# Attention with top-32 masks and a gated product: the order and the engines of the weight decoding at the start, and the place of a small addition

## The chip, the cores and the metric

One core of a Trainium2 chip. The metric is the device time of one execution in microseconds (us); the median of three executions of the kernel before is 1266.33 us (1266.02 to 1269.22).

The engines are TensorE (PE in the rows, its weight loads PEld), VectorE (DVE), ScalarE (ACT), GpSimd (POOL) and SyncE (SP, which issues the DMAs). Each runs its own instructions strictly in the order in which the program lists them.

## What is computed

```
scores = q @ k.T / 8                       # 8 batches, 8 heads, 576 tokens, 64 wide
scores = where(scores >= 32nd largest of its row, scores, -1e9)
attn   = exp(scores - rowmax);  attn /= sum(attn) + 1e-9
x      = (attn @ v), heads side by side    # 4608 x 512
h      = (x @ w1) * (x @ w2) @ w3          # w1, w2: 512 x 1024, w3: 1024 x 1024
out    = h @ w_out                         # 1024 x 512
```

All of it is in 32-bit floating point.

## The kernel before, in words

**Slots.** The attention is cut into 144 slots, 18 to a batch; a slot is 128 query rows of two heads. Four consecutive rounds of the main loop (line 529) carry a slot: its scores (TensorE, `scores`), its search for the 32 largest (VectorE, `top32_steps`, tile `w` and `top`), its mask and exponentials (GpSimd and ScalarE, `edges_of`, `mask`, `exps`, tile `pab`), and its transposition and product with v (TensorE, `turn`, `values`). So in the round in which VectorE searches slot p, GpSimd and ScalarE mask slot p-1. In that round GpSimd forms the `edge` of slot p-1 first, then two subtractions on `pab`, then `over`, later the addition of 1e-9 to the two sums (`enlarge`, line 310, called at line 581), and, once VectorE has inverted the sums (`invert`), two multiplications (`normalise`). The next `edge` needs the end of VectorE's next search.

**Gated product.** The products with w1, w2 and the folded w3 @ w_out (`moe_steps`) are fed to TensorE in portions behind the attention, three portions in a round (`fill`, `SHARE`). Each product is made of three matmuls, from high parts and rests (`wh` and `wl` for w1 and w2, `wf` for the fold), since an fp32r operand carries only a high part. The evictions of a portion (`take_a`, `take_b`) come at the start of the next; the last of these is a subtraction on GpSimd into tile `g`.

**Weights.** The weights enter as 64-bit words in 40 units of 128 x 512: 8 of w_out, 16 of w3, 16 of w1 and w2. A unit is a generator of steps (`decode`, line 113). With `by_pool`, GpSimd first makes the sign bits (tile `y`); then ScalarE makes two conversions (`t`, into PSUM, and `r`, in the place of the word, tile `z`); then VectorE combines (SCALAR_TENSOR_TENSOR into `y`), preceded by the sign (TENSOR_SCALAR) where `by_pool` is false; then GpSimd adds (TENSOR_TENSOR into `y` or `wo`). A w1 or w2 unit goes on with the high part on ScalarE (`wh`, line 151) and the rest, `y` minus `wh`, on GpSimd (`wl`, line 153). A w3 unit waits for its four products with w_out (`product`, line 172, tile `pf`); after the second unit of a block ScalarE takes the high part and VectorE the rest (`wf`).

**What orders them.** `warm` (line 514) is called up to five times a round; a call is a turn. In a turn a new unit may enter if fewer than five are under way, and every unit under way takes its next step:

```
        if fetched and (n % 5 if n < 11 else n % 2) and len(going) < 5:
            z, step = fetched.pop(0)
            going.append(step(z))
        going[:] = [unit for unit in going if next(unit, "end") != "end"]
        prefetch(3)
```

`prefetch` issues the DMA of the next units on SyncE's queue, four buffers `z` in all. `weigh` (line 161) issues queued products of w3, 1 in the middle of a round and up to 8 at its end. The first portion of the gated product is issued once all 8 blocks of the fold and the first halves of w1 and w2 are in (`done`). In the kernel before, 12 of the 40 signs are made on GpSimd (those of every second unit of w_out and w3), and all 16 rests of w1 and w2.

A slot is numbered here by its place, 0 to 143. Slot k begins on VectorE with the first `w<-s,st`, and on GpSimd with its `edge`.

Of the kernel before, what the change touches and what calls it, by code (L numbers as in the profile page):

```python
# [9 lines left out]
F32 = mybir.dt.float32  # L10
# [4 lines left out]
ALU = mybir.AluOpType  # L15
# [6 lines left out]
NCC, NFC, NEC = DM // 128, DF // 128, DM // 128  # L22
# [13 lines left out]
STEEP = 2.0**80  # L36
SCALE = 0.125
AHEAD = 3
SHARE = 3520, 3520, 3200


# [19 lines left out]
def attn_moe(ctx: ExitStack, tc: tile.TileContext, q, k, v, w1, w2, w3, w_out, out, flag, general):  # L61
# [12 lines left out]
    pe, act, dve, pool, sp = nc.tensor, nc.scalar, nc.vector, nc.gpsimd, nc.sync  # L74
# [24 lines left out]
    wo = const.tile([128, NFC * DM], F32, tag="wl1", name="wo")  # L99
# [4 lines left out]
    if not general:  # L104
        pe, act, dve, pool, sp = (InOrder(tc, e) for e in (pe, act, dve, pool, sp))

    def fetch(src):

        z = z_p.tile([128, 1024], F32, tag="z", name="z")
        sp.dma_start(z.bitcast(I32), src)  # L110
        return z
# [27 lines left out]

    done = {"pf": 0, 0: 0, 1: 0}  # L140

    def load_w12(i, c, z):
        y = yield from decode(z, False)
        c, h = c // 2, c % 2
        if len(wl[i]) == h:
            while done["pf"] < NFC:
                yield
        if len(wl[i]) == h:
            wl[i].append(const.tile([128, half], F32R, tag="wl1", name="wl11"))
        y_hi, y_lo = wh[i][:, c * DF + h * 512 : c * DF + (h + 1) * 512], wl[i][h][:, c * 512 : (c + 1) * 512]  # L150
        act.copy(y_hi, y)
        yield
        pool.tensor_tensor(y_lo, y, y_hi.bitcast(F32), op=ALU.subtract)
        done[h] += 1

    def load_wout(c, z):
        yield from decode(z, c % 2, wo[:, c * 512 : (c + 1) * 512])

    fold, heavy = {}, []

    def weigh(n):
        while heavy and n:
            heavy.pop(0)()
            n -= 1

    def load_w3(c, z):
        f, i = c // 2, c % 2
        y = yield from decode(z, i)
        if i == 0:
            fold[f] = ps_m.tile([128, 512], F32, tag="mm", name=f"pf{f}")  # L170

        def product(j):
            pe.matmul(
                fold[f], y[:, (j % 4) * 128 : (j % 4 + 1) * 128], wo[:, j * DM : (j + 1) * DM],
                start=(j == 0), stop=(j == NFC - 1),
            )

        heavy.extend((lambda j=j: product(j)) for j in range(4 * i, 4 * i + 4))
        last = heavy[-1]
        if general:  # L180
            weigh(4)
        while last in heavy:
            yield
        if i == 1:
            cut = slice(f * DM, (f + 1) * DM)
            act.copy(wf[0][:, cut], fold[f])
            yield
            dve.tensor_tensor(wf[1][:, cut], fold[f], wf[0][:, cut].bitcast(F32), op=ALU.subtract)
            done["pf"] += 1
# [120 lines left out]
    def enlarge(sums):  # L310
        pool.tensor_scalar(sums, sums, 1e-9, None, op0=ALU.add)
# [56 lines left out]
    def moe_steps(b, part, xs, after):  # L368
# [57 lines left out]
            after(lambda p=p, e=e: take_o(p, e))  # L426
            yield cost

    outs_w = [(w_out[c], lambda z, c=c: load_wout(c, z)) for c in range(8)]
    thirds = [(w3[c], lambda z, c=c: load_w3(c, z)) for c in range(2 * NFC)]  # L430
    firsts = [
        (w[2 * c + h], lambda z, i=i, c=2 * c + h: load_w12(i, c, z))
        for h in range(2) for i, w in enumerate((w1, w2)) for c in range(NCC)
    ]
    startup = outs_w[:4] + thirds[:1] + outs_w[4:] + thirds[1:2]
# [1 line left out]
        startup += firsts[f - 1 : f] + thirds[2 * f : 2 * f + 2]  # L437
    startup += firsts[NFC - 1 :]

    def new_x():  # L440
        return x_p.tile([128, 2, NA], F32R, tag="x", name="xf")

    if general:
        for src, step in startup:
            for _ in step(fetch(src)):
                pass
        with tc.For_i(0, B, 1) as b:
            seen = small.tile([1, 1], I32, tag="seen", name="seen", bufs=1)
            nc.sync.dma_start(seen, flag[ds(b + 1, 1), :])
            with tc.If(nc.values_load(seen, min_val=0, max_val=1) > 0):  # L450
                for part in range(2):
                    qk, vts, xs = {}, {}, {}
                    for of, hps, t in SLOTS:
                        if of != part:
                            continue
                        for hp in hps:
                            if hp not in qk:
                                qk[hp], vts[hp], xs[hp] = load_qk(b, part, hp), load_v(b, hp), new_x()
                        s, st = new_s(), scores([qk[hp] for hp in hps], t)
                        for h in range(2):  # L460
                            take_scores(s, st, h)
                        edge = top32_exact(s)
                        pab, sums = new_weights()
                        for a in range(2):
                            mask(s, edge, pab, a)
                            exps(edge, pab, sums, a)
                        enlarge(sums)
                        invert(sums)
                        normalise(pab, sums)
                        tp, ro = turn(pab)  # L470
                        ov = values([vts[hp] for hp in hps], t, *take_turned(tp, ro), ro)
                        to = places([xs[hp] for hp in hps], t)
                        take_high(to, ov)
                        take_low(to, ov)
                    for _ in moe_steps(b, part, [xs[hp] for hp in range(NHP)], lambda f: f()):
                        pass
        return
# [26 lines left out]
                spare -= cost  # L504

    waiting = list(startup)
    fetched, going, turns = [], [], []

    def prefetch(n):
        while waiting and len(fetched) < n:  # L510
# [3 lines left out]
    def warm(first=True):  # L514

        if p < 0 and not first:
            return
        turns.append(p)
        n = len(turns)
        if fetched and (n % 5 if n < 11 else n % 2) and len(going) < 5:  # L520
            z, step = fetched.pop(0)
            going.append(step(z))
        going[:] = [unit for unit in going if next(unit, "end") != "end"]
        prefetch(3)

    qk[units[0]] = load_qk(*units[0])
# [1 line left out]
    n_slots = len(slots)  # L528
    for p in range(-1, n_slots + 3):
        i, j, m = p + 1, p - 1, p - 2  # L530
        if i < n_slots:
            for u in units:
                if first[u] - 2 == i:
                    qk[u] = load_qk(*u)
                if first[u] == i:
                    vts[u] = load_v(u[0], u[2])
        finder = top32_steps(ss[p], *sts.pop(p), p) if 0 <= p < n_slots else iter(())
        if 0 <= j < n_slots:
            edges[j] = edges_of(j)
        next(finder, None)  # L540
        if m - 1 in lows:
            take_low(*lows.pop(m - 1))
            b, part, _ = slots[m - 1][0][0]
            if final[b, part] == m - 1:
                queue.append(moe_steps(b, part, [xts.pop((b, part, hp)) for hp in range(NHP)], put_off.append))
        next(finder, None)
        if p >= 0:
            warm()
        if 0 <= j < n_slots:
            pabs[j] = new_weights()  # L550
            for a in range(2):
                mask(ss[j], edges[j], pabs[j][0], a)
            compare(j)
        fill(SHARE[0])
        next(finder, None)
        if 0 <= m < n_slots:
            tp, ro = turn(pabs[m][0])
            pts, pr = take_turned(tp, ro)
        warm(False)
        if 0 <= j < n_slots:  # L560
            exps(edges[j], *pabs[j], 0)
            exps(edges[j], *pabs[j], 1)
        weigh(1)
        fill(SHARE[1])
        next(finder, None)
        warm(False)
        if i < n_slots:
            st = scores([qk[u] for u in slots[i][0]], slots[i][1])
            ss[i] = new_s()
            take_scores(ss[i], st, 0)  # L570
            sts[i] = st, take_scores(ss[i], st, 1)
        if 0 <= m < n_slots:
            us, t = slots[m]
            for u in us:
                if u not in xts:
                    xts[u] = new_x()
            ov = values([vts[u] for u in us], t, pts, pr, ro)
            lows[m] = places([xts[u] for u in us], t), ov
            take_high(*lows[m])
        if 0 <= j < n_slots:  # L580
            enlarge(pabs[j][1])
        next(finder, None)
        warm()
        next(finder, None)
        if 0 <= j < n_slots:
            invert(pabs[j][1])
            normalise(*pabs[j])
        weigh(8)
        fill(SHARE[2])
        for _ in finder:  # L590
            pass
        if 0 <= m < n_slots:
            del ss[m], pabs[m], edges[m]
        warm()
# [62 lines left out]
```

## Time and profile before

| | |
|---|---|
| median of three executions | 1266.33 us |
| profiled execution, its own time | 1266.87 us |
| its span, first to last instruction | 1264.9 us |
| mean granted clock of TensorE | 0.991 of full speed |
| busy TensorE / VectorE / ScalarE / GpSimd | 1209.7 / 1135.0 / 943.4 / 872.4 us |
| TensorE in 40 slices of 31.6 us, busy tenths | 3788889999..., and 9 in nearly all slices after |
| slot 0 begins on VectorE, slot 18 | at 9.57 us, at 208.15 us |

A busy tenth of 9 means 90% or more. Busy matmul time is modelled to the end of the pipeline, so a slice in which TensorE shows 8 may hold real gaps. In the tables of groups, a row gives engine, operation, output and inputs, sizes and count, then busy us in all and mean ns of one, then the engine's idle time just before them and what ended it.

### The profile page before, as it was taken

The page shows a single profiled execution, that of the slowest core. Times are in us where ns is not written, and L with a number is a line of the kernel's source. Part 1 is how long each engine was busy: PE and PEld are TensorE (multiplying, and loading weights), DVE is VectorE, ACT ScalarE, POOL GpSimd, SP SyncE. Part 2 cuts the span into 40 slices and gives each one's busy share as a digit, 9 for nine tenths or more (in the row PEclk, how much of TensorE's full clock was granted, in tenths as well). Part 3 has the DMA queues.
Part 4 walks back from the last instruction along what each step waited for, and adds up shares of the span by engine and source line. Part 5 has one row for each costly group of instructions (what it writes and reads, how often), then busy time and mean ns, then how long its engine had stood idle before and what let it go on. Part 6 is the DMA issues. An engine that isn't in the chain of part 4 may idle for free.

```text
span 1264.9 us, 29916 instructions
## 1 busy us (share of the span) xinstructions
PE 1209.7 (96%) x10513; PEld 1043.5 (82%) x10513; DVE 1135.0 (90%) x3968; ACT 943.4 (75%) x2025; POOL 872.4 (69%) x1213
## 2 busy tenths in 40 slices
PE   3788889999999999999999999999999999999998
PEld 1444568888888888888888888888888888888898
DVE  7897979999999999999999999999999999999910
ACT  5887877777777777777777777777777777777731
POOL 5887887676766767676766767676766767676731
PEclk9999989999999999999999999999999999999999
DMA  7533421202112121202112121202112111202000
GB/s 236 174 129 130 156 70 40 91 27 70 55 39 90 36 63 40 90 28 70 55 39 91 36 63 40 90 28 70 55 39 91 35 63 40 91 27 70 13 22 21
DMA packets 42803, 85.92 MB, mean 68 GB/s; under 512 B 4754, under 2 KB 21138, under 8 KB 42642
## 3 DMA queue, kind: packets, MB, share of 16 engines
q1 hardware_dynamic: 42642, 83.91, 20.6%
q8 instruction: 85, 1.39, 0.5%
q14 instruction: 76, 0.62, 0.2%
HBM read 74.45 MB, written 9.44 MB: 66 GB/s over the span
## 4 chain that ended last, share of the span: by engine, by line
PE 75%; POOL 10%; DVE 7%; ACT 4%; issue 3%; DMA 1%; SPq 0%; DVEq 0%; POOLq 0%; ACTq 0%
PE ab L52 27%; PE eo L52 15%; PE ro L52 12%; PE st L52 11%; PE tp L52 9%; POOL pab L52 5%; DVE w L52 3%; DVE top L52 2%; ACT pab L52 2%; PE pf L52 2%; POOL y L52 2%; POOL g L52 1%; DVE y L52 1%; POOL wl L52 1%; ACT pts L52 1%
## 5 line engine op out<-in xcount | busy, mean ns | idle before, releaser
L52 POOL TENSOR_TENSOR pab<-s,pab 128x576 f32<-128x576 f32 x288 | 404.8, 1427 | 121.9 <-ACT pab L52 121.9
L52 DVE MAX8 top<-w 128x8 f32<-128x192 f32 (+1 forms) x1152 | 478.5, 448 | 0.0
L52 PE MATMUL ab<-xf,wh 128*128 128x256 f32 (+1 forms) x2048 | 438.5, 302 | 10.1 <-DVE y L52 8.7
L52 PEld LDWEIGHTS ab<-xf,wh 128*128 128x128 f32 x2048 | 332.9, 189 | 21.6 <-DVE y L52 9.5
L52 ACT ACTIVATE pab<-s,edge 128x576 f32<-128x576 f32 x288 | 208.0, 769 | 176.6 <-POOL edge L52 176.6
L52 PE MATMUL ab<-xf,wl 128*128 128x256 f32 (+1 forms) x1024 | 307.4, 300 | 0.0
L52 DVE MATCH_REPLACE8 w<-top,w 128x192 f32<-128x192 f32 x864 | 289.7, 343 | 0.0
L52 POOL TENSOR_SCALAR pab<-pab,sums 128x576 f32<-128x576 f32 x288 | 212.6, 751 | 78.0 <-DVE sums L52 78.0
L52 ACT ACTIVATE pab<-pab,edge 128x576 f32<-128x576 f32 x288 | 223.1, 779 | 11.9 <-POOL pab L52 9.7
L52 PE MATMUL eo<-g,wf 128*128 128x256 f32 (+1 forms) x1536 | 231.6, 301 | 0.0
L52 PEld LDWEIGHTS eo<-g,wf 128*128 128x128 f32 x1536 | 208.5, 188 | 8.1 <-issue 7.5
L52 PEld LDWEIGHTS ab<-xf,wl 128*128 128x128 f32 x1024 | 193.4, 189 | 4.1 <-issue 4.1
L52 PE MATMUL st<-kt,qt 64*128 64x192 f32 (+3 forms) x1280 | 182.8, 435 | 9.8 <-DMA kt<-in_k 4.8
L52 ACT COPY pts<-tp 128x1024 f32<-128x1024 f32 x144 | 145.6, 1011 | 46.8 <-PE tp L52 44.3
L52 ACT COPY s<-st 128x768 f32<-128x768 f32 (+1 forms) x288 | 169.9, 646 | 5.8 <-PE st L52 5.8
L52 PE MATMUL tp<-ident,pab 128*128 128x128 f32 x1152 | 153.8, 278 | 14.2 <-DVE w L52 9.5
L52 PEld LDWEIGHTS st<-kt,qt 64*128 64x128 f32 (+1 forms) x1280 | 97.9, 178 | 83.7 <-issue 18.6
L52 DVE TENSOR_TENSOR w<-w,st 128x384 f32<-128x384 f32 x288 | 158.2, 549 | 4.9
L52 PE MATMUL ro<-pts,vt 128*64 128x128 f32 (+1 forms) x2560 | 161.2, 269 | 1.0 <-ACT pr L52 1.0
L52 DVE TENSOR_TENSOR w<-s,st 128x384 f32<-128x384 f32 x288 | 146.7, 551 | 14.0
L52 POOL TENSOR_TENSOR g<-whole,g 128x256 fp32r<-128x256 f32 (+1 forms) x128 | 103.3, 807 | 78.6 <-ACT g L52 78.6
L52 PEld LDWEIGHTS ro<-pts,vt 128*64 128x64 f32 x2560 | 127.5, 137 | 34.4 <-issue 24.2
(47 smaller groups left out, 1128.7 us busy)
## 6 DMA issues: line engine op xcount, KB each, us to landing
vt<-in_v SPq DMA_DIRECT2D x64, 352.0 KB, 3.2
kt<-in_k SPq DMA_DIRECT2D x64, 320.0 KB, 3.8
z<-in_w SPq DMA_DIRECT2D x32, 512.0 KB, 3.8
qt<-in_q SPq DMA_DIRECT2D x32, 160.0 KB, 3.2
out_t<-osb SPq DMA_DIRECT2D x32, 160.0 KB, 1.8
z<-in_wo SPq DMA_DIRECT2D x8, 512.0 KB, 5.2
qt<-in_q SPq DMA_DIRECT2D x32, 128.0 KB, 3.1
out_t<-osb SPq DMA_DIRECT2D x32, 128.0 KB, 1.7
```

The source lines that it names most:

```text
L52: ins = fn(*args, **kw)
```

## The change

The turns in which a unit enters are read from a list of ones and zeros, one digit a turn; a second list says for each unit, in its order of entry, whether GpSimd makes its sign (29 ones of 40); a third says for each unit of w1 and w2 whether VectorE makes its rest (12 ones of 16). The order of the units is changed at two places and among the last nine. In the middle of a round 2 queued products of w3 are issued in place of 1. The addition of 1e-9 to the sums is called right behind the exponentials, ahead of the evictions of the second portion and of two turns that stood before it.

```diff
+ENTER = "011111010110010011111101000100110101111011001101110111011111000111100010000101010101010101010101010101010101010101010101"
+BY_POOL = "1111011100011100111001110101011111111111"
...
-    def load_w12(i, c, z):
-        y = yield from decode(z, False)
+    def load_w12(i, c, z, by_pool, rest):
+        y = yield from decode(z, by_pool)
...
-        pool.tensor_tensor(y_lo, y, y_hi.bitcast(F32), op=ALU.subtract)
+        (dve if rest else pool).tensor_tensor(y_lo, y, y_hi.bitcast(F32), op=ALU.subtract)
...
-    def load_wout(c, z):
-        yield from decode(z, c % 2, wo[:, c * 512 : (c + 1) * 512])
+    def load_wout(c, z, by_pool):
+        yield from decode(z, by_pool, wo[:, c * 512 : (c + 1) * 512])
...
-    def load_w3(c, z):
+    def load_w3(c, z, by_pool):
...
-        y = yield from decode(z, i)
+        y = yield from decode(z, by_pool)
...
-        (w[2 * c + h], lambda z, i=i, c=2 * c + h: load_w12(i, c, z))
+        (w[2 * c + h], lambda z, s, i=i, c=2 * c + h: load_w12(i, c, z, s, '1101011101011111'[8 * h + 4 * i + c // 2] == "1"))
...
+    startup = [startup[i] for i in [0, 1, 2, 3, 4, 5, 6, 7, 8, 9, 11, 10, 12, 13, 14, 16, 15, 17, 18, 19, 20, 21, 22, 23, 24, 25, 26, 27, 28, 29, 30, 31, 33, 35, 32, 38, 39, 37, 34, 36]]
...
-        if fetched and (n % 5 if n < 11 else n % 2) and len(going) < 5:
+        if fetched and ENTER[n : n + 1] != "0" and len(going) < 5:
             z, step = fetched.pop(0)
-            going.append(step(z))
+            by_pool = BY_POOL[len(entered)] == "1"
+            entered.append(n)
+            new = step(z, by_pool)
...
             exps(edges[j], *pabs[j], 1)
-        weigh(1)
+            enlarge(pabs[j][1])
+        weigh(2)
         fill(SHARE[1])
...
-        if 0 <= j < n_slots:
-            enlarge(pabs[j][1])
         next(finder, None)
```

How this moves instructions is shown at three places. The first is VectorE at the start of the program, up to the search of slot 0 (`top_98` is the tile of slot 0's largest values, `y` and `t` belong to weights). Before:

```order
L52 TENSOR_SCALAR y<-t 128x512
L52 SCALAR_TENSOR_TENSOR y<-t,y 128x512
L52 TENSOR_TENSOR w<-s,st 128x2x192 x2
L52 TENSOR_TENSOR w<-w,st 128x2x192 x2
L52 MAX top_98<-w 128x8 x2
```

Now:

```order
L54 TENSOR_TENSOR w<-s,st 128x2x192 x2
L54 TENSOR_TENSOR w<-w,st 128x2x192 x2
L54 SCALAR_TENSOR_TENSOR y<-t,y 128x512
L54 MAX top_98<-w 128x8 x2
L54 MATCH_REPLACE w<-top_98,w 128x192 x2
```

The sign of the first unit is gone from VectorE, and its combination stands behind the first four operations of the search.

The second is GpSimd in slot 11, from its edge to the next (`wl` is a rest of w1, TENSOR_SCALAR `y<-z` a sign, TENSOR_TENSOR `y<-y,z` the addition of a unit). Before:

```order
L52 TENSOR_TENSOR edge<-top_100,coef 128x4
L52 TENSOR_TENSOR wl_107<-y,wh_101 128x512
L52 TENSOR_TENSOR y<-y,z 128x512
L52 TENSOR_TENSOR pab<-s,pab 128x576 x2
L52 TENSOR_TENSOR over<-top_100 128x2
L52 TENSOR_TENSOR wl_107<-y,wh_101 128x512
L52 TENSOR_TENSOR y<-y,z 128x512
L52 TENSOR_SCALAR sums<-sums 128x2
L52 TENSOR_SCALAR pab<-pab,sums 128x576 x2
L52 TENSOR_TENSOR wl_107<-y,wh_101 128x512
L52 TENSOR_TENSOR y<-y,z 128x512
L52 TENSOR_TENSOR edge<-top_98,coef 128x4
```

Now:

```order
L54 TENSOR_TENSOR edge<-top_100,coef 128x4
L54 TENSOR_SCALAR y<-z 128x512
L54 TENSOR_TENSOR pab<-s,pab 128x576 x2
L54 TENSOR_TENSOR over<-top_100 128x2
L54 TENSOR_TENSOR wl_107<-y,wh_101 128x512
L54 TENSOR_SCALAR y<-z 128x512
L54 TENSOR_SCALAR sums<-sums 128x2
L54 TENSOR_SCALAR y<-z 128x512
L54 TENSOR_TENSOR y<-y,z 128x512
L54 TENSOR_SCALAR y<-z 128x512
L54 TENSOR_SCALAR pab<-pab,sums 128x576 x2
L54 TENSOR_TENSOR y<-y,z 128x512
```

Three rests and three additions have become one rest, two additions and four signs.

The third is GpSimd in slot 15, after the last weights. Before:

```order
L52 TENSOR_TENSOR edge<-top_98,coef 128x4
L52 TENSOR_TENSOR pab<-s,pab 128x576 x2
L52 TENSOR_TENSOR over<-top_98 128x2
L52 TENSOR_TENSOR g<-whole,g 128x320
L52 TENSOR_SCALAR sums<-sums 128x2
L52 TENSOR_SCALAR pab<-pab,sums 128x576 x2
```

Now:

```order
L54 TENSOR_TENSOR edge<-top_98,coef 128x4
L54 TENSOR_TENSOR pab<-s,pab 128x576 x2
L54 TENSOR_TENSOR over<-top_98 128x2
L54 TENSOR_SCALAR sums<-sums 128x2
L54 TENSOR_TENSOR g<-whole,g 128x320
L54 TENSOR_SCALAR pab<-pab,sums 128x576 x2
```

The addition to the sums has passed the subtraction into `g`.

## Rows read from the trace of the kernel before

**Rows 1.** The page: busy time, and TensorE in 40 slices.

```profile
PE 1209.7 (96%) x10513; PEld 1043.5 (82%) x10513; DVE 1135.0 (90%) x3968; ACT 943.4 (75%) x2025; POOL 872.4 (69%) x1213
...
PE   3788889999999999999999999999999999999998
```

**Rows 2.** Windows: stretch and length, busy PE, PEld, DVE, ACT, POOL, granted clock, DMA.

```profile
9.57:192.35 182.78, 143.17 (x844) 88.50 (x845) 162.99 (x494) 140.03 (x276) 151.53 (x175) 0.94 0.43 142
600.00:640.00 40.00, 40.00 (x340) 35.39 (x338) 37.84 (x133) 31.29 (x68) 28.82 (x41) 1.00 0.17 53
1220.00:1240.00 20.00, 20.00 (x161) 19.94 (x160) 2.51 (x7) 4.34 (x11) 2.94 (x4) 1.00 0.05 19
```

**Rows 3.** Timeline of VectorE: start, length, operation, idle before and its end.

```profile
8.24 0.69 DVE L52 TENSOR_SCALAR y<-t 128x512 int32<-128x512 int32 x1 [8.24 <-ACT t L52]
...
9.57 1.01 DVE L52 TENSOR_TENSOR w<-s,st 128x384 f32<-128x384 f32 x2
...
20.24 1.01 DVE L52 TENSOR_TENSOR w<-s,st 128x384 f32<-128x384 f32 x2
...
49.93 0.69 DVE L52 SCALAR_TENSOR_TENSOR y<-t,y 128x512 int32<-128x512 int32 x1 [2.47 <-POOL y L52]
...
53.24 1.01 DVE L52 TENSOR_TENSOR w<-s,st 128x384 f32<-128x384 f32 x2
```

**Rows 4.** Timeline of ScalarE at the start.

```profile
6.50 1.18 ACT L52 COPY s<-st 128x768 f32<-128x768 f32 x2 [4.49 <-PE st L52]
7.57 0.64 ACT L52 ACTIVATE t<-z 128x512 f32<-128x512 f32 x1
...
8.68 0.62 ACT L52 ACTIVATE t<-z 128x512 f32<-128x512 f32 x1
```

**Rows 5.** Groups of VectorE, by form, from 0 to 200 us.

```profile
L52 DVE SCALAR_TENSOR_TENSOR y<-t,y 128x512 int32<-128x512 int32 x40 | 27.6, 689 | 6.6 <-POOL y L52 3.2 <-ACT xf L52 2.5
L52 DVE TENSOR_SCALAR y<-t 128x512 int32<-128x512 int32 x28 | 19.1, 683 | 14.1 <-ACT t L52 13.9
...
L52 DVE TENSOR_TENSOR wf<-pf,wf 128x512 fp32r<-128x512 f32 x8 | 5.5, 686 | 1.3 <-ACT wf L52 1.3
```

**Rows 6.** Groups of GpSimd, by form, from 0 to 200 us.

```profile
L52 POOL TENSOR_TENSOR pab<-s,pab 128x576 f32<-128x576 f32 x32 | 44.6, 1416 | 8.1 <-ACT pab L52 8.1
L52 POOL TENSOR_TENSOR y<-y,z 128x512 int32<-128x512 int32 x32 | 41.5, 1298 | 1.3 <-ACT z L52 1.1
...
L52 POOL TENSOR_TENSOR wl<-y,wh 128x512 fp32r<-128x512 f32 x16 | 20.5, 1280 | 4.7 <-ACT wh L52 4.7
...
L52 POOL TENSOR_SCALAR y<-z 128x512 f32<-128x512 f32 x12 | 7.9, 660 | 8.1 <-DMA z<-in_wo 8.1
...
L52 POOL TENSOR_TENSOR over<-top 128x2 f32<-128x2 f32 x16 | 3.2, 200 | 0.0
```

**Rows 7.** Timeline of GpSimd: the edges of slots 11 and 14.

```profile
145.21 0.20 POOL L52 TENSOR_TENSOR edge<-top,coef 128x4 f32<-128x4 f32 x1
...
185.01 0.21 POOL L52 TENSOR_TENSOR edge<-top,coef 128x4 f32<-128x4 f32 x1
```

**Rows 8.** Groups of ScalarE, by form, from 0 to 200 us: an exponential has two instructions.

```profile
L52 ACT ACTIVATE pab<-pab,edge 128x576 f32<-128x576 f32 x32 | 24.7, 775 | 4.5 <-POOL pab L52 4.1
...
L52 ACT ACTIVATION_READ_ACCUMULATOR pab<-pab,edge 128x1 f32 x32 | 6.2, 193 | 0.0
```

**Rows 9.** Waits of VectorE and GpSimd in slots 0 to 15: us in total, times, longest.

```profile
DVE y L52 <- ACT t L52: 5.7, 4, 2.3
...
DVE y L52 <- POOL y L52: 3.2, 2, 2.5
...
POOL sums L52 <- ACT pab L52: 2.0, 5, 0.8
```

**Rows 10.** Waits from 240 to 1160 us.

```profile
DVE sums L52 <- POOL sums L52: 21.7, 40, 0.9
...
PE tp L52 <- DVE w L52: 0.7, 4, 0.2
```

More of the change, by code (lines that the diff above doesn't have):

```diff
@@ L427, in moe_steps @@
             yield cost
-    outs_w = [(w_out[c], lambda z, c=c: load_wout(c, z)) for c in range(8)]
-    thirds = [(w3[c], lambda z, c=c: load_w3(c, z)) for c in range(2 * NFC)]
+    outs_w = [(w_out[c], lambda z, s, c=c: load_wout(c, z, s)) for c in range(8)]
+    thirds = [(w3[c], lambda z, s, c=c: load_w3(c, z, s)) for c in range(2 * NFC)]
     firsts = [
-        (w[2 * c + h], lambda z, i=i, c=2 * c + h: load_w12(i, c, z))
+        (w[2 * c + h], lambda z, s, i=i, c=2 * c + h: load_w12(i, c, z, s, '1101011101011111'[8 * h + 4 * i + c // 2] == "1"))
         for h in range(2) for i, w in enumerate((w1, w2)) for c in range(NCC)
@@ L444, in attn_moe @@
         for src, step in startup:
-            for _ in step(fetch(src)):
+            for _ in step(fetch(src), False):
                 pass
@@ L506, in attn_moe @@
     waiting = list(startup)
-    fetched, going, turns = [], [], []
+    fetched, going, turns, entered, begun = [], [], [], [], []
     def prefetch(n):
@@ L519, in warm @@
         n = len(turns)
-        if fetched and (n % 5 if n < 11 else n % 2) and len(going) < 5:
+        if fetched and ENTER[n : n + 1] != "0" and len(going) < 5:
             z, step = fetched.pop(0)
-            going.append(step(z))
-        going[:] = [unit for unit in going if next(unit, "end") != "end"]
+            by_pool = BY_POOL[len(entered)] == "1"
+            entered.append(n)
+            new = step(z, by_pool)
+            if False:
+                next(new)
+                begun.append(new)
+            else:
+                going.append(new)
+        going[:] = [unit for unit in going if next(unit, "end") != "end"] + begun
+        begun.clear()
         prefetch(3)
```

## The prediction, made before the changed kernel was run

> **What bounds the kernel now.** I read the page first. TensorE is busy in nearly every slice but the first six; all its missing tenths lie in the first 190 us, the stretch in which weights enter [rows 1]. The windows say what that means on either side. Between 600 and 640 us TensorE is busy 40.00 of 40.00 us while VectorE has 37.84 and GpSimd 28.82, and near the end TensorE works alone, 20.00 of 20.00 [rows 2]. After the weights TensorE is therefore the bound, and from 240 to 1160 us the trace has 0.7 us in which it waited for anything [rows 10]. In the first stretch, 9.57 to 192.35 us, no engine is full: of 182.78 us VectorE is busy 162.99, GpSimd 151.53, TensorE 143.17, ScalarE 140.03 [rows 2]. Sixteen slots take these 182.78 us, 11.4 each, against 7.9 later. Nothing but the first stretch can pay. Since both programs begin the gated product in the same slot, with the same number of matmuls in each slot and in the tail, a microsecond saved before TensorE fills up is a microsecond off the end.
>
> In that stretch VectorE and GpSimd are tied to each other twice a slot: GpSimd's edge needs VectorE's last search step, and VectorE's inversion needs the sums from GpSimd. So a slot takes about the longer of the two engines' work, plus what the ties leave open: VectorE has 182.78 - 162.99 = 19.8 us open, in waits such as 5.7 us for ScalarE's `t` and 3.2 us for a sign from GpSimd [rows 2, 9].
>
> **The change part by part.**
>
> *Work moved.* 17 signs leave VectorE at 0.683 us and come to GpSimd at 0.660: -11.6 and +11.2. 12 rests leave GpSimd at 1.280: -15.4. What a rest costs on VectorE no row shows. The nearest row is the rest of the fold, same shape and same subtraction on the same engine, with one input from PSUM: 0.686 us. The far bound is GpSimd's own 1.280 [rows 5, 6]. I take 0.69, since engine and operation are the same, so +8.3 on VectorE, and keep 1.28 for the range. In all GpSimd loses 4.2 us and VectorE 3.3 in a stretch where both are nearly full. The rest of the forecast is about where that work lies.
>
> *A, slots 0 to 3.* VectorE now waits 8.24 us for the first `t`, makes a sign and a combination, and begins the search at 9.57 [rows 3]. In the changed order the search stands first, and the score copies that it needs end at 6.50 + 1.18 = 7.68 [rows 4]: -1.9. Slot 0 then holds six weight operations as before, and may keep its 10.67 us (20.24 - 9.57). Slot 1 holds three in place of five: two at 0.65 (between a row's mean and its pace back to back), -1.3. In slot 3 VectorE waited 2.47 us for a sign that GpSimd had reached late [rows 3]; of the two units with a sign from GpSimd that slot 3 combines now, one has it ahead of the masks and the other is combined one search step later, so -2.5. Against this, ScalarE gets a fifth pair of conversions ahead of the scores of slot 1; a pair takes 8.68 - 7.57 = 1.1 us [rows 4], +1.1. Sum: **-4.6**, to be seen at the start of slot 4, now 53.24. The cautious end is what GpSimd's own work in slots 0 to 2 loses: from 4 signs, 9 additions, 1 rest to 5 signs and 8 additions, 0.66 - 1.30 - 1.28 = -1.9.
>
> *B, slots 3 to 10.* GpSimd's list goes from 6 signs, 20 additions, 7 rests (38.9 us with rows 6) to 14, 22 and 2 (40.4): **+1.5**. VectorE's list stays at 41 or 42 weight operations. This is where the saving of signs is paid back.
>
> *C, slots 11 to 13.* From the edge of slot 11 to that of slot 14 passed 185.01 - 145.21 = 39.8 us [rows 7]. GpSimd had 7 additions and 8 rests there, 7 x 1.30 + 8 x 1.28 = 19.3 us; now 5 signs, 5 additions, 2 rests, 12.4 us. That is -6.9. In the last of the three, VectorE's search beside it (7.5 without weights, 37.84 us of 40 in a slot of 7.9, and one rest) is then longer than GpSimd's 7.1 by 1.1. **-5.8**.
>
> *D, the addition to the sums.* It now stands right behind the exponentials. GpSimd must wait for the second of them, 0.775 + 0.193 us after the last mask, less the 0.20 of `over`, so 0.8 us [rows 6, 8], wherever no operation of a weight stands between. That is so in four of slots 0 to 13 (1, 3, 6, 13): +3.2, where 2.0 us were waited before [rows 9]: **+1.2**. Behind it now queue the subtraction into `g` and the steps of two turns, which get later by no more; their readers are turns away. In the other 130 slots the same move is put at nothing: it shortens VectorE's wait for the sums (21.7 us from 240 to 1160), but TensorE covers all of that, and if it did not, 21.7 us would be the gain [rows 10].
>
> *At nothing.* Two products in mid-round in place of one: their number is the same, and TensorE has 39.6 us open in the stretch [rows 2]. Were it not covered, one product more in mid-round would hold up scores, not the sum. SyncE's queue: the loads of q and k stand behind one load of weights less; the loads of weights wait for a free `z` as before, and the first addition, which frees one for the fifth unit, is delayed by little more than the two signs that now stand ahead of it (1.3 us).
>
> Sum: -4.6 + 1.5 - 5.8 + 1.2 = **-7.7 us**. The profiled execution took 1266.87, the median 1266.33, 0.5 less; I put the sum on the median: **1258.6 us**.
>
> **The rivals.**
>
> *Slower: the two engines shut each other out.* Of VectorE's operations in the stretch, none subtracts or compares two tensors that both lie in SBUF; each has PSUM on one side or a single input. The moved rest reads `y` and `wh`, both in SBUF, while GpSimd is busy 83% of the time reading SBUF. If the two cannot read together, a rest waits for half of GpSimd's operation in flight, up to 1.416 / 2 = 0.71 us [rows 6], and GpSimd then stands for 0.69: 1.4 x 12 = 16.8 us, all on the path if neither engine has room. -7.7 + 16.8 = +9.1, **1275.4 us**. It decides from 0.64 us lost per rest. No row of before has such an operation, so the trace neither shows nor excludes it. For it speaks that both engines are nearly full; against it that VectorE and GpSimd have 20 and 31 us open in the stretch, in which part of such waits would fall, and that the twelve rests are spread over nine slots.
>
> The Trainium skill (SBUF — State Buffer, "Who interferes with whom") says just this: a VectorE instruction with two SBUF inputs contends with a GpSimd instruction that reads SBUF, and the second to issue waits until the first is finished. By that page the sum would be the rival's, +9.1, where the row of the fold's rest gives -7.7; no run here shows it yet.
>
> *No change that can be told: a rest costs what it cost GpSimd, and A stays small.* With 1.28 in place of 0.69 a rest costs 7.1 us more in all, half of it in slots where VectorE is the longer, 3.5; and A is only GpSimd's -1.9, because ScalarE or the loads hold up the start. -1.9 + 1.5 - 5.8 + 1.2 + 3.5 = -1.5, **1264.8 us**. For it speaks that slot 2 now holds more of GpSimd's work (3 signs and 4 additions) than before.
>
> *Much faster: VectorE runs without gaps.* If the new order also fills the 19.8 us, VectorE's load alone is the limit: -19.8 - 3.3 = -23.1, **1243.2 us**. Against it: its waits come from ScalarE and GpSimd alike [rows 9], and in some slots four pairs of conversions, 4 x 1.1 us, now stand on ScalarE.
>
> *The change does nothing:* if a unit of the last list were still needed later than before, the gated product would begin later. It begins in the same slot, so this has no chance of its own.
>
> **How the numbers follow.** A difference of 0.3%, 3.8 us, is about what a measurement of this kernel can tell from no change. Forecast as worked out, faster by 4 to 15 us: 0.58. Much faster: 0.11. No change: 0.17. Shut out, or another mishap above +3.8: 0.14. So faster 0.69, same 0.17, slower 0.14. The range reaches below to half of VectorE's gaps, -7.7 - 9.9 and the 1.9 by which A might be larger, near **1247**; above it takes in the rival of no change with its bound and part of the way to the slower one, **1269**. Left out are most of the slower rival and the end of the fastest case.
>
> **What would show it.** In the profile of the changed kernel: slot 4 begins on VectorE near 48.6 us (A); the edges of slots 11 and 14 lie 34 us apart (C); VectorE's rest takes about 0.69 us and GpSimd's operations keep their lengths (against the slower rival); TensorE is full from about 185 us, and the tail is the same. The forecast is wrong if the rests on VectorE show 1 us or more or a wait for GpSimd in front of each, if GpSimd's subtractions on `pab` lengthen beyond 1.42 us, if VectorE's wait for signs grows well beyond 3.2 us, or if TensorE waits after 200 us.

## The result, and the profile after

The changed kernel takes **1247.44 us** (median of four executions, 1246.48 to 1248.36), the kernel before 1266.70 beside it: ratio 0.9844, interval 0.9827 to 0.9861. That is faster by 19.3 us. The forecast was 7.7 us, that is 1258.6; the time lies in the range (1247 to 1269) at its lower end, and the size of the gain was wrong by more than half.

The profiled execution took 1246.48 us, with a span of 1244.6 where before it was 1264.9. The page answers to [rows 1], and its chain of work is given for the first time here:

```profile
PE 1202.3 (97%) x10513; PEld 1042.5 (84%) x10513; DVE 1137.1 (91%) x3963; ACT 941.0 (76%) x2025; POOL 869.4 (70%) x1218
...
PE   4889799999999999999999999999999999999998
...
PE 91%; DVE 3%; POOL 2%; ACT 2%; issue 1%; DMA 1%; SPq 0%; ACTq 0%; DVEq 0%
```

In the kernel before, that chain ran 75% over TensorE, 10% over GpSimd and 7% over VectorE. The windows answer to [rows 2]: the first stretch, slots 0 to 15 by their starts on VectorE, and the same 40 us later:

```profile
6.86:177.71 170.85, 138.45 (x836) 86.31 (x837) 164.23 (x490) 141.51 (x280) 150.72 (x181) 0.96 0.47 157
...
600.00:640.00 40.00, 40.00 (x356) 35.53 (x352) 38.74 (x137) 31.26 (x68) 28.69 (x42) 1.00 0.16 49
```

The stretch is 11.9 us shorter, yet VectorE's work in it grew from 163.0 to 164.2 us. What went are VectorE's open times: 170.85 - 164.23 = 6.6 us, before 19.8. From 600 to 640 us TensorE shows 40.00 of 40.00 busy, to the digit what it showed before.

The starts of slots on VectorE and the edges on GpSimd answer to [rows 3, 7]. VectorE:

```profile
6.86 1.02 DVE L54 TENSOR_TENSOR w<-s,st 128x384 f32<-128x384 f32 x2 [6.86 <-ACT s L54]
...
47.91 1.01 DVE L54 TENSOR_TENSOR w<-s,st 128x384 f32<-128x384 f32 x2
...
177.71 1.02 DVE L54 TENSOR_TENSOR w<-s,st 128x384 f32<-128x384 f32 x2
...
1175.10 1.02 DVE L54 TENSOR_TENSOR w<-s,st 128x384 f32<-128x384 f32 x2
```

GpSimd, slots 11 and 14:

```profile
138.01 0.20 POOL L54 TENSOR_TENSOR edge<-top,coef 128x4 f32<-128x4 f32 x1
...
171.21 0.20 POOL L54 TENSOR_TENSOR edge<-top,coef 128x4 f32<-128x4 f32 x1
```

From slot 16 to slot 143 (the last of these starts) pass 997.4 us, and 1003.4 before: 6.0 us less, in a part of the program in which nothing but the place of the small addition changed.

The groups of VectorE and GpSimd from 0 to 200 us answer to [rows 5, 6]. VectorE, with the rests that it now makes:

```profile
L54 DVE TENSOR_TENSOR wl<-y,wh 128x512 fp32r<-128x512 f32 x12 | 13.3, 1110 | 0.1
...
L54 DVE TENSOR_TENSOR wf<-pf,wf 128x512 fp32r<-128x512 f32 x8 | 5.5, 682 | 0.0
```

GpSimd:

```profile
L54 POOL TENSOR_TENSOR pab<-s,pab 128x576 f32<-128x576 f32 x36 | 51.6, 1458 | 6.9 <-ACT pab L54 6.9
...
L54 POOL TENSOR_TENSOR over<-top 128x2 f32<-128x2 f32 x18 | 5.4, 297 | 0.0
...
L54 POOL TENSOR_TENSOR wl<-y,wh 128x512 fp32r<-128x512 f32 x4 | 5.2, 1288 | 0.0
```

A rest on VectorE takes 1.11 us on average, not 0.69, and GpSimd's operations beside it are longer: `pab` 1.458 (1.416 before), `over` 0.297 (0.200).

The waits from 7 us to slot 16 answer to [rows 9]. VectorE:

```profile
DVE w L54 <- ACT s L54: 6.9, 1, 6.9
DVE y L54 <- ACT t L54: 3.5, 6, 1.0
DVE y L54 <- POOL y L54: 0.8, 1, 0.8
DVE sums L54 <- POOL sums L54: 0.6, 1, 0.6
```

GpSimd:

```profile
POOL sums L54 <- ACT pab L54: 5.9, 9, 1.7
```

The wait for `s` is the one ahead of slot 0. GpSimd waits 5.9 us for exponentials (before 2.0), more than the 3.2 forecast for the moved addition, but VectorE does not feel it: its own wait for the sums is 0.6 us here and was 3.7 in the same slots before.

### The profile page after: what moved, and what is told of

The parts are those of the page before. It is cut to its first block, busy times and chain, and to the rows that moved or that the text cites. A ratio compares the mean times of both kernels' runs of the same rounds, so it can differ in the third digit from the quotient of the medians.

```text
span 1244.6 us, 29906 instructions
## 1 busy us (share of the span) xinstructions
PE 1202.3 (97%) x10513; PEld 1042.5 (84%) x10513; DVE 1137.1 (91%) x3963; ACT 941.0 (76%) x2025; POOL 869.4 (70%) x1218
## 4 chain that ended last, share of the span: by engine, by line
PE 91%; DVE 3%; POOL 2%; ACT 2%; issue 1%; DMA 1%; SPq 0%; ACTq 0%; DVEq 0%
PE ab L54 33%; PE eo L54 17%; PE ro L54 15%; PE st L54 13%; PE tp L54 10%; PE pf L54 3%; POOL pab L54 1%; DVE w L54 1%; DVE top L54 1%; DVE y L54 1%; DVE wl L54 1%; POOL y L54 1%; ACT pab L54 0%; POOL wo L54 0%; ACT s L54 0%
## 5 line engine op out<-in xcount | busy, mean ns | idle before, releaser
L54 PEld LDWEIGHTS tp<-ident,pab 128*128 128x128 f32 x1152 | 133.8, 142 | 24.7 <-POOL pab L54 15.4
```

The costliest lines, as they stand in the source:

```text
L54: ins = fn(*args, **kw)
```

## Experiments

Three questions came from this. Why do the later slots gain? Why did VectorE's waits vanish? What lengthens the rests? Two theories stand in several expectations. **P** says that the place of the addition pays in every slot after the weights, behind a TensorE that only looks full. **M** says that the list of turns and the list of signs fit each other, so that either without the other loses. Each expectation spells out its theories and rivals. "After" is the changed kernel.

### The place of the addition

*e1: the kernel before with this edit alone.*

```diff
             exps(edges[j], *pabs[j], 1)
+            enlarge(pabs[j][1])
...
-        if 0 <= j < n_slots:
-            enlarge(pabs[j][1])
```

> The kernel before with one edit, the addition of 1e-9 called right behind the exponentials. Theory P (place): in the slots after the weights the change made a slot 7.864 us long in place of 7.899, because the subtraction into g no longer delays the normalised weights and with them TensorE's transposes; this is the whole of that gain and comes from this edit alone: 0.035 x 126 = 4.4 us, so about 1262 us, and transposes spaced 7.86 us apart in every slot. Rival Q: the shorter slots come from another phase of the engines that the start leaves behind; then this edit alone gives 0 +- 1 us, 1266 us.

Measured: 1261.92 us, ratio 0.9965 (0.9953 to 0.9976). The first stretch stayed at 182.86 us; slots 16 to 143 took 997.28, that is 6.1 less. This edit alone makes the gain, as P says; that every slot shares in it does not hold, as shown below.

*e2: after, with the addition in its old place* (the same edit backwards).

> The changed kernel with the addition of 1e-9 at its old place. Theory P: slots of 7.90 us again, about 4.4 us slower than 1247.4, so 1252; and GpSimd's waits for the exponentials at the start (6.7 us) fall back to about 2, with no gain in time since VectorE is the bound there. Rival Q: 1247 to 1248.

Measured: 1254.64 us, ratio 0.9905 (0.9889 to 0.9922), 7.2 above after. Slots 16 to 143 are back at 1003.23, and the first stretch is 2.85 longer. In the new order the addition pays at the start too; in the old one (e1) it did not.

The traces show how. `tp`, the tile of the transposes, and `st`, the scores, share their PSUM buffers (tag "a", in `turn` and `scores`), and the first step of the search still reads `st`. So the transposes need the first step of VectorE's next slot to be over. GpSimd before, in a slot in which it has a subtraction into `g`:

```profile
710.90 0.19 POOL L52 TENSOR_TENSOR over<-top 128x2 f32<-128x2 f32 x1
712.21 0.74 POOL L52 TENSOR_TENSOR g<-whole,g 128x256 fp32r<-128x256 f32 x1 [1.12 <-ACT g L52]
713.04 0.21 POOL L52 TENSOR_SCALAR sums<-sums 128x2 f32<-128x2 f32 x1
```

VectorE before, then TensorE before:

```profile
711.93 0.75 DVE L52 MAX8 top<-w 128x8 f32<-128x576 f32 x1
713.29 0.17 DVE L52 RECIPROCAL sums<-sums 128x2 f32<-128x2 f32 x1 [0.60 <-POOL sums L52]
713.37 0.74 DVE L52 MAX8 top<-w 128x8 f32<-128x576 f32 x1
714.21 1.02 DVE L52 TENSOR_TENSOR w<-s,st 128x384 f32<-128x384 f32 x2
```

```profile
712.07 3.14 PE L52 MATMUL eo<-g,wf 128*128 128x256 f32 x24
715.38 1.06 PE L52 MATMUL tp<-ident,pab 128*128 128x128 f32 x8 [0.17 <-DVE w L52]
```

The addition queues behind the subtraction, which stands 1.12 us for ScalarE; VectorE then stands 0.60 us; the first step of its next slot ends at 715.23, and the transposes start at 715.38. In a like slot after, GpSimd, VectorE and TensorE:

```profile
410.95 0.21 POOL L54 TENSOR_SCALAR sums<-sums 128x2 f32<-128x2 f32 x1 [1.21 <-ACT pab L54]
411.24 0.73 POOL L54 TENSOR_TENSOR g<-whole,g 128x256 fp32r<-128x256 f32 x1
```

```profile
412.20 1.02 DVE L54 TENSOR_TENSOR w<-s,st 128x384 f32<-128x384 f32 x2
```

```profile
412.02 3.14 PE L54 MATMUL eo<-g,wf 128*128 128x256 f32 x24
415.00 1.03 PE L54 MATMUL tp<-ident,pab 128*128 128x128 f32 x8
```

Here VectorE's step ends at 413.22, well ahead of the transposes. The same 24 matmuls show 3.14 us in both. But the transposes start 3.31 us after their start before and 2.98 after. The modelled end of the matmuls had covered 0.16 of the 0.33 us, so the profile named a wait of only 0.17, and 0.7 us of such waits in all [rows 10]. Over the 117 slots from 240 to 1160 us, the time from the start of the last run of matmuls (those in a row on the same tiles) to the transposes is 0.952 us on average before and 0.921 after (e2: 0.959, e1: 0.920). That is 0.031 x 117 = 3.6 us; the transposes there follow each other after 7.901 us on average before and 7.864 after, which is 0.037 x 117 = 4.3 us less in all.

This gain does not lie in every slot. A batch has 18 slots. From 240 to 1160 us the time from one slot's transposes to the next one's falls by 0.35, 0.18 and 0.06 us in three of them, and changes by 0.03 or less in the others. Behind a run of 24 matmuls as shown above, which comes 7 times in the 117 slots, the transposes start 0.32 us sooner on average, and where two matmuls with `wh` stand last, 19 times, 0.07. So TensorE does cover the late addition in most slots, and VectorE still waits for the sums after, shorter at a time:

```profile
DVE sums L54 <- POOL sums L54: 17.7, 44, 0.5
```

Before these were 21.7 us, the longest 0.9 [rows 10].

### The lists

*e3: after, with one product of w3 in mid-round*, `weigh(1)` for `weigh(2)`.

> The changed kernel with 1 product of w3 in mid-round in place of 2. If ScalarE's waits for the fold's products, 8.1 us before and 1.0 now, went because of this, they come back and VectorE waits behind them: 3 to 6 us slower, 1250 to 1253. If they went with the turns, no change: 1247.

Measured: 1246.99 us, ratio 0.9839 (0.9823 to 0.9856): no difference from after. ScalarE's wait for the fold's products stays at 1.0 us.

*e4: after, with the signs of before.*

```diff
-        y = yield from decode(z, by_pool)
+        y = yield from decode(z, False)
...
-        yield from decode(z, by_pool, wo[:, c * 512 : (c + 1) * 512])
+        yield from decode(z, c % 2, wo[:, c * 512 : (c + 1) * 512])
...
-        y = yield from decode(z, by_pool)
+        y = yield from decode(z, i)
```

> The changed kernel with the signs made as before, 12 on GpSimd and 28 on VectorE. Theory S (VectorE's load is what counts at the start): VectorE has hardly a gap there now (6.6 us of 170.9), so 17 signs of 0.68 us more on it cost nearly all of their 11.6 us: about 1258 us. Rival L (the turns count, not the load): waits of 13 us went because the units enter at better turns; then this costs 3 us or less, 1250 us or below.

*e6: after, with the turns of before.*

```diff
-        if fetched and ENTER[n : n + 1] != "0" and len(going) < 5:
+        if fetched and (n % 5 if n < 11 else n % 2) and len(going) < 5:
```

> The changed kernel with the rule of entry of the kernel before, so that the units enter in other turns, signs and rests staying where the change put them. Rival L: most of the 13 us of VectorE's waits come back, 1257 to 1262 us. Theory S: the load is the same, and no more than 4 us come back, 1248 to 1251 us.

*e8: both edits at once.*

> The changed kernel with both the turns of entry and the signs of before; rests on VectorE, the moved addition and the order of units stay. Theory M (the lists are matched: each alone undone cost 22 and 25 us, more than the whole gain): undone together they cost less than the sum of 46, since the old turns go with the old signs: about 1262 (the kernel before with the moved addition alone) plus what the rests cost VectorE there (12 x 1.1 us) less what GpSimd saves, so 1258 to 1268. Rival N (the costs add): 1247 + 22 + 25 = 1294.

Measured: e4 1269.15 us, ratio 1.0018 (1.0008 to 1.0027); e6 1272.21, 1.0047 (1.0030 to 1.0063); e8 1269.17, 1.0016 (1.0005 to 1.0028). Undoing one list costs 21.7 or 24.8 us, undoing both 21.7, where a plain sum would have been 46.5. S and L both priced e4 and e6 too low, by 10 us and more: neither the load nor the turns alone explains them. M comes within 1.2 us of e8 (1258 to 1268), N (1294) is far off. And e8 differs from e1 only by the rests, the order of the units and the product in mid-round, yet is about 7 us slower: beside the old lists these parts lose time. The windows of the first stretch, of e4 and then of e6:

```profile
9.07:199.57 190.50, 148.69 (x835) 90.25 (x836) 175.11 (x506) 140.33 (x277) 140.20 (x164) 0.89 0.42 136
```

```profile
6.78:201.88 195.10, 145.89 (x827) 87.67 (x828) 164.74 (x489) 141.03 (x278) 151.07 (x181) 0.92 0.42 137
```

The old signs give VectorE 10.9 us more work and leave 15.4 us open, where after has 6.6. The old turns leave its work as it is (164.7) and 30.4 us open. In e6 ScalarE stands in front of the fold. Its waits before, in after and in e6:

```profile
ACT wf L52 <- PE pf L52: 8.1, 3, 4.7
```

```profile
ACT wf L54 <- PE pf L54: 1.0, 1, 1.0
```

```profile
ACT wf L54 <- PE pf L54: 24.4, 6, 7.2
```

Each of ScalarE's operations for a weight stands in one queue with the conversions and exponentials of the slot, so a wait for products of w3 there holds up what stands behind it: in e6 VectorE waits 9.7 us for ScalarE's `wf` and 4.5 for its `wh`, in after for neither. The turns decide whether this wait comes up: with the new ones it is 1.0 us (after, e3) and 0.9 (e4), with the old ones 8.1 (before), 24.4 (e6) and 11.9 (e8). e3 shows that the number of products in mid-round does not. In e4 this wait is small, so the time that the old signs cost does not come from it.

*e7: after, with the units in the old order* (the line that rearranges `startup` is left out).

> The changed kernel with the units in the order of before; the lists of turns, signs and rests stay, so some of their digits fall on other units. If the order of the units carries part of the gain: 2 to 6 us slower, 1249 to 1253. If it only names units that are alike: 1247 to 1248.

Measured: 1251.49 us, ratio 0.9877 (0.9861 to 0.9894), 4.0 above after; open time on VectorE 10.6 us. The interval just touches that of after, so the 4 us are at the edge of what these runs can tell. Since the digits of the lists fall on other units here, the run shows that order and lists belong together, not what the order is worth by itself.

*e5: after, with all 16 rests on GpSimd* (the digits of the third list all zero).

> The changed kernel with all 16 rests on GpSimd. Theory X (the two engines shut each other out): VectorE's rest took 1.11 us in the mean, up to 2.12, where the fold's rest takes 0.68, and GpSimd's subtractions on the masks took 1.458 in place of 1.416; with the rests gone these fall back to 0.68 and 1.42. Time: GpSimd gains 15.4 us of rests and loses about 4 us of blocking, VectorE loses 13.3 us; if GpSimd is then the longer, 4 to 8 us slower, 1251 to 1255. Rival Y (the rests on VectorE were a loss): 2 to 5 us faster, 1243 to 1245.

Measured: 1253.19 us, ratio 0.9888 (0.9872 to 0.9905), 5.7 above after. X forecast this (1251 to 1255). VectorE has 11.0 us less work and 25.1 us open. Slots 10 and 11 of e5, the same of after, then VectorE's waits in the first stretch of e5:

```profile
114.31:126.73 12.42, 10.42 (x53) 5.36 (x52) 9.90 (x31) 9.53 (x19) 12.25 (x15) 1.00 0.32 106
126.73:138.82 12.09, 10.99 (x60) 6.28 (x58) 9.72 (x31) 10.64 (x21) 11.93 (x15) 1.00 0.66 222
```

```profile
112.36:123.48 11.12, 10.50 (x54) 5.49 (x53) 11.09 (x32) 9.21 (x19) 10.70 (x15) 1.00 0.42 134
123.48:135.99 12.51, 9.71 (x57) 5.57 (x55) 12.37 (x34) 10.67 (x21) 9.83 (x12) 1.00 0.65 222
```

```profile
DVE y L54 <- ACT t L54: 12.9, 14, 2.5
DVE sums L54 <- POOL sums L54: 7.7, 4, 4.8
```

In e5 GpSimd is busy 12.25 of 12.42 us and 11.93 of 12.09, and VectorE 9.90 and 9.72. In after VectorE is the fuller engine, with 11.09 of 11.12 and 12.37 of 12.51. So it is not room on VectorE that makes the moved rests pay; they take the fullness from GpSimd. That VectorE's longer waits for `t` (12.9 us, 3.5 in after) go back to GpSimd too is likely, but not shown.

*e9: before, with the lists of turns and signs alone* (rests on GpSimd, units, products and addition as before).

> The kernel before with the two lists of turns and signs alone: all rests on GpSimd, the addition at its old place, one product in mid-round, units in the old order. If what the parts cost when undone adds up (rests 5.7, addition 7.2, unit order 4.0, product 0): 1247.4 + 16.9 = 1264. If these two lists carry the start by themselves: 1253 to 1256.

Measured: 1261.45 us, ratio 0.9961 (0.9947 to 0.9976). This lies between the two expectations, nearer to the cautious one: the two lists do not carry the gain by themselves. VectorE waits 13.4 us for the sums, with GpSimd full in slots 10 to 13 as in e5 (51.6 us busy of 52.3 in e9, 52.4 of 53.0 in e5).

*e12: after, with all 40 signs on GpSimd* (`BY_POOL` all ones).

> The changed kernel with all 40 signs on GpSimd: the 11 that VectorE still makes move too. Load alone (VectorE's work is what the start costs): VectorE loses 11 x 0.68 = 7.5 us and GpSimd, with 18 us open in the stretch, takes 7.3 more: 1240 to 1243. Matched lists (a unit whose sign is on GpSimd takes one turn more, so moving 11 signs moves 11 units against the turns, and GpSimd fills up in the last weight slots as it did with the rests on it): VectorE's gaps grow from 6.6 to 15 us or more and the time is the same or up to 10 us longer, 1247 to 1257.

Measured: 1251.86 us, ratio 0.9875 (0.9858 to 0.9891), 4.4 above after; the interval overlaps that of after a little. VectorE has 3.3 us less to do and 9.2 us more open (15.8), as the matched lists forecast; its waits for signs are 3.8 us (0.8 in after), those for `t` 7.5 (3.5).

### What a rest costs beside GpSimd

*e10: a kernel that leaves out the whole computation* and only runs 24 operations in a row: VectorE's subtraction 128x512 with both inputs in SBUF, the same with one in PSUM, GpSimd's subtraction 128x576, and pairs of them at once.

> Leaves out the whole computation; measures what a rest costs on VectorE: runs of 24 subtractions of 128x512 on VectorE, with both inputs in SBUF or one in PSUM, alone and beside 24 of GpSimd's 128x576 subtractions, and single-input searches beside them. Theory X (shut out): alone both forms take 0.68 us and GpSimd's 1.42; together the form with two SBUF inputs is stretched to about the length of GpSimd's operation (they take turns, a pair 2 us or more), while the form with PSUM and the search stay at their lengths and GpSimd at 1.42. Rival: VectorE's 1.11 us in the changed kernel came from waiting for a semaphore or a buffer; then all forms keep their lengths together.

Measured, in the timeline of one execution of 233.81 us: first each alone, then the pair with both inputs in SBUF, then the pair with one in PSUM.

```profile
9.65 17.41 DVE L54 TENSOR_TENSOR low<-y,h 128x512 fp32r<-128x512 f32 x24 [9.65 <-ACT h L54]
...
29.98 17.37 DVE L54 TENSOR_TENSOR low<-yp,h 128x512 fp32r<-128x512 f32 x24 [2.92 <-ACT yp L54]
...
49.08 35.34 POOL L54 TENSOR_TENSOR m<-s,m 128x576 f32<-128x576 f32 x24 [48.64 <-ACT yp L54]
...
86.13 42.20 DVE L54 TENSOR_TENSOR low<-y,h 128x512 fp32r<-128x512 f32 x24 [38.79 <-ACT h L54]
86.73 42.86 POOL L54 TENSOR_TENSOR m<-s,m 128x576 f32<-128x576 f32 x24 [2.32 <-ACT yp L54]
...
131.80 17.36 DVE L54 TENSOR_TENSOR low<-yp,h 128x512 fp32r<-128x512 f32 x24 [3.46 <-ACT yp L54]
131.91 35.45 POOL L54 TENSOR_TENSOR m<-s,m 128x576 f32<-128x576 f32 x24 [2.32 <-ACT yp L54]
```

Alone, a rest takes 17.41 / 24 = 0.73 us whichever the memory. Beside GpSimd, the form with two SBUF inputs takes 42.20 / 24 = 1.76, and GpSimd 42.86 / 24 = 1.79 in place of 1.47; the form with one PSUM input changes nothing. So theory X holds in kind; a pair takes 1.8 us, where X said 2 or more. The searches ran beside the second half of the last GpSimd row shown, at 17.45 / 24 = 0.73 us each, and it kept its length.

*e11: after, with ScalarE copying the unit to PSUM, from where VectorE makes the rest.*

```diff
+        if rest:
+            yp = ps_m.tile([128, 512], F32, tag="mm", name="yp")
+            act.copy(yp, y)
...
+            dve.tensor_tensor(y_lo, yp, y_hi.bitcast(F32), op=ALU.subtract)
```

> The changed kernel, but for the 12 rests on VectorE ScalarE first copies the unit into PSUM, and VectorE subtracts from there. Theory X: VectorE's rest falls from 1.11 to 0.69 us and GpSimd's subtractions from 1.458 to 1.42, 5 us off VectorE and 4 off GpSimd; ScalarE gets 12 x 0.6 = 7 us more, for which it has room in most slots: 1243 to 1246. Against it: three PSUM buffers are shared with the decoding and the products, and a fourth user makes units wait: 1249 or more.

Measured: 1253.54 us, ratio 0.9902 (0.9885 to 0.9918), 6.1 above after. The conflict is gone, in VectorE's groups and GpSimd's:

```profile
L54 DVE TENSOR_TENSOR wl<-yp,wh 128x512 fp32r<-128x512 f32 x12 | 8.2, 684 | 2.8 <-ACT yp L54 2.8
```

```profile
L54 POOL TENSOR_TENSOR pab<-s,pab 128x576 f32<-128x576 f32 x36 | 50.2, 1417 | 9.8 <-ACT pab L54 9.8
```

VectorE's work fell by 4.1 us, but its open time rose by 6.9. It waits 2.8 us for the copies and 7.0 for `t` (3.5 in after). The copies add 5.7 us to ScalarE's work in the stretch and share PSUM buffers (tag "mm") with `t`; ScalarE's `t` waits 2.4 us for VectorE's rests, in after not at all. No run was faster than the changed kernel beyond the intervals.

## Why the prediction was wrong in size

e2 separates the terms: it holds A, B and C, and after adds D to it. The marks of A, B and C are the starts of slots 0, 4 and 16 on VectorE and the edges of slots 11 and 14 on GpSimd. Read in e2, those edges are at 140.03 and 173.25 us, and those starts at 6.89, 48.91 and 180.59; B is then 140.03 - 48.91 = 91.12 us against 145.21 - 53.24 = 91.97 before.

| term | forecast | measured |
|---|---|---|
| A, to the start of slot 4 | -4.6 | 48.91 - 53.24 = -4.3 |
| B, slot 4 to the edge of slot 11 | +1.5 | -0.9 |
| C, edge of slot 11 to that of slot 14 | -5.8 | 33.22 - 39.80 = -6.6 |
| edge of slot 14 to slot 16 | 0 | 7.34 - 7.34 = 0.0 |
| D, the addition, first stretch | +1.2 | 170.85 - 173.70 = -2.9 |
| D, slots 16 to 143 | 0 | 997.40 - 1003.23 = -5.8 |

**The failed step is D.** It was put at +1.2 us at the start and "at nothing" in the other 130 slots, "but TensorE covers all of that". It measured -8.7 in all, 9.9 of the 12.6 us by which the forecast missed the span (-20.3 against -7.7). These are the two profiled executions; by the medians of e2 and after, D is worth 7.2 us, and in the order of before 4.9 (e1). The row with 40.00 of 40.00 was read as proof of cover, and the row with 0.7 us of waits as a second one. Both rest on modelled ends of matmuls, and so are one proof, not two. The prediction itself named the price of being wrong, "21.7 us would be the gain", but no rival carried it. What came was neither nothing nor 21.7: the cover fails in three of a batch's 18 slots and holds, to 0.03 us, in the others.

**A and C held**, by place and size. After itself begins slot 4 at 47.91 us (forecast near 48.6), and its edges lie 33.2 us apart (forecast 34). Two parts of A held by themselves: in e2 slot 1 is 1.3 us shorter (forecast 1.3) and slot 3 is 2.3 (2.5). The rest of its fit is luck: slot 0 begins 2.7 us sooner (1.9) and is 1.9 longer (1.1). In the last interval of C, VectorE is the longer engine as forecast (8.89 us of 9.03 in e2, GpSimd 7.30).

**B had the wrong sign.** It was priced by GpSimd's list of work, 38.9 to 40.4 us, as if that engine could lose no wait. VectorE was open 8.8 us in slots 4 to 10 before (80.68 - 71.90 between the starts of slots 4 and 11) and 1.6 in after (75.57 - 73.97).

**Work and waits both missed, against each other.** VectorE's load was forecast 3.3 us lower; it is 1.2 higher, chiefly since twelve rests cost 12 x (1.11 - 0.69) = 5.0 more. Its waits were left standing but for slot 3's; 13.2 of 19.8 us went. That is the mechanism of the much faster rival ("VectorE runs without gaps", 1243.2 us, chance 0.11), as far as the waits go. Its reason against, that the waits come from ScalarE and GpSimd alike, is true and was no obstacle: the list of turns alone, taken back, leaves 30.4 us open on VectorE (e6). e4, e6 and e8 show that turns and signs must fit each other; e5 shows that the rests must leave GpSimd as well, and e9, which lacks the addition and the order of units too, agrees.

**The slower rival's mechanism is real, its price was not.** A rest meets GpSimd and takes up to 2.12 us (the one at 129.20 us), and GpSimd's operations stretch; both were named in advance as signs against the forecast. The loss was put at 1.4 us a rest, all on the path. VectorE lost 0.42, and moving the rests still gained 5.7 us (e5), since a rest on GpSimd stood where GpSimd was full. The Trainium skill (SBUF — State Buffer, "Who interferes with whom") is borne out on who meets whom: two SBUF inputs beside a GpSimd read conflict, one PSUM input does not. Full exclusion, as it states it, does not fit e10: the pairs ended 129.59 - 86.13 = 43.5 us after the first start, where one after the other would be 17.4 + 35.3 = 52.7. Whether a part of each operation is exclusive and the rest is not, e10 cannot tell.

**At nothing, rightly:** the second product in mid-round (e3). The order of units, given no price of its own, costs about 4 us when it alone is taken back (e7).

What stays open: which single digit of the lists removes which wait. They were tried only as wholes. Nor was it tried why the earlier addition gains 2.9 us in the first stretch of the new order and nothing in that of the old. A rival that no run holds fixed is TensorE's clock: in the first stretch the granted clock was 0.94 of full speed before and 0.96 in after, 0.92 in e2 and e6, 0.89 in e4. How much of their times it makes, and how much it only follows, is not shown.

## What to carry to other kernels

A row that shows an engine fully busy with modelled ends does not prove cover: compare the starts of the same run of matmuls and of what follows it, in slots with and without the suspect ahead. Do this for each kind of slot, since cover can hold in most and fail in a few. A small operation on which another engine waits belongs ahead of anything in its queue that may stand for a third engine. When work is moved between two nearly full engines, price the waits of both as well as the work, and expect the parts of a schedule not to add: take one back at a time, and also two together.

## What was not expected of the hardware

With both inputs in SBUF, VectorE's 128x512 subtraction went from 0.73 to 1.76 us beside GpSimd's 128x576 subtraction, and that from 1.47 to 1.79; each pair took 1.8 us where the two one after the other take 2.2. VectorE paid most of it. In the kernel even GpSimd's smallest operation shows it: `over` on 128x2 went from a mean of 0.200 to 0.297 us, since four of its 18 took 0.64 to 0.68; in e11, with the rests from PSUM, the mean is 0.197.
